# A radix-4 even half, a new front order and a table of vector shares in a kernel that mixes a spectral filter with a state-space recurrence

## The chip, the core and the metric

The kernel runs on one NeuronCore of one Trainium2 chip. Its engines work at the same time, each through a queue of its own in program order: TensorE (PE in the profile, its weight loads PEld), VectorE (DVE), ScalarE (ACT), GpSimd (POOL) and SyncE (SP), which here only issues DMAs. They meet through semaphores. The metric is device time of one execution in microseconds (us); lower is better. The time before is 340.28 us, the median of 3 runs (340.24 to 340.29).

## What is computed

One input x of 2048 tokens by 1024 channels goes two ways, and a gate per token mixes the results:

```python
g = sigmoid((x * gate_w).sum(-1, keepdims=True))
# way A: a filter in the two-dimensional spectrum
X = rfft2(x.astype(float32), axes=(-2, -1))
a = irfft2(X * (w_r + 1j * w_i), s=(S, D), axes=(-2, -1)).astype(bfloat16)
# way B: a diagonal complex recurrence over the tokens, P = 1024 states
Lam_bar = exp(dt * Lam);  B_bar = ((Lam_bar - 1.0) / Lam)[:, None] * Bmat
Bu = einsum("bld,pd->blp", x, B_bar)
h[t] = Lam_bar * h[t-1] + Bu[t]
b = 2.0 * einsum("blp,dp->bld", h, Cmat).real + x * Dskip
out = g * a + (1 - g) * b
```

Shapes: S = 2048, D = 1024; inputs and output are bfloat16.

## The kernel before, in words

**Way A** is done with matrix products. The *front* treats 16 row groups j = 0..15 of 128 tokens. For each, `turn_x(j)` (L663) transposes the group with 8 TensorE transposes into `pt`, and ScalarE copies it out into `xQ` (L667), from where way B reads x too. `fold(j)` (L670) makes on VectorE the sums and the differences of the lower and the upper 512 channels: two instructions of 512 elements (L674, L675) into `preT`. `fd(j)` (L342) is the transform along d: the sums go against a matrix for the even frequencies and the differences against one for the odd ones, 4 matmuls of 512 columns each (L346), and one copy of 1024 elements out of PSUM into `X1` (L349; on VectorE for j = 3, 5, 7, else on ScalarE). `s1(j)` (L352) is the first step of the transform along the tokens, 4 matmuls on half the rows (L358); its result `A1` is copied out by VectorE for j < 8 and by ScalarE from 8 on (L363) and goes to DRAM by a DMA of SP (L365, tile `turn_scratch`). From j = 8 on, `A1` lives in four rotating buffers, so A1 of j = 12 waits until the store of j = 8 has landed and until VectorE has kept a column of it (`keep_A1`, L371). `fd` and `s1` share two PSUM buffers (`psA`): each waits until what stood in its buffer two uses ago has been copied out.

**Way B** has 8 chunks c of 256 tokens. `unit(c, q)` (L301) yields two *halves*: 32 matmuls of 256 columns each (L308, tile `psu`), copied out by ScalarE (L310, tile `h`). A half needs its four transposed parts of B (`BT`, DMA transposes of SP, L207). After the second half, `recur` (L254) appends the chunk's recurrence as a list of pieces for VectorE: multiplications by tables of sines and cosines (L263, L266), additions, scans (L278). `vector(us)` (L321) takes pieces from this list, in order, until the sum of their listed costs reaches what is owed; `c_half(tb)` (L574), 16 matmuls against C and 4 for the skip term, first takes all pieces of its chunk that are left (`vector_until`, L330). So where `vector` is called and with how much sets where the recurrence stands in VectorE's queue. `early(tb)` makes output tiles 0..9 ahead, `own_tile` the last ones.

**The tables** come from `make_tab(jp)` for four groups jp (L210). Each is a chain that goes from VectorE (angles, L215; range reduction, L828, L830) to ScalarE (L832, L833, L835 and the scaled copies `t`, L226, L231) and back (tab, L232, L237). Its tiles have one buffer, so a table starts after the one before it has been read. It is cut by `yield`s into about four pieces, which the loop over the front hands out. Ahead of the tables, a small version of the same chain (`sincos` on `ang2`, L844) and some 24 tiny VectorE operations (L847 to L869) make the factors per state.

**The order around the change.** TensorE, VectorE and ScalarE run in the order in which the program is written; the DMAs of SP and POOL are ordered by the framework's scheduler. The front is a loop (L872) that calls `front()` for j = 0..15. `plan` gives for each j the order of F (`fd(j+1)`), S (`s1(j)`), T (the next `turn_x`) and f (the next `fold`), and `order` the loads that follow it: parts of B, later parts of C (L563, also DMA transposes of SP, which may only write where A1 of j < 8 was stored). A half of way B follows each j from 8 on, and `vector(4.2)` each from 9 on. `T2` (tile `raw`) is the matrix of `s1`, loaded in three parts. After the front come the middle part of way A (`step()`) with halves, `early` tiles and `vector` calls between its steps, and the closing loop. The first instruction after the front's last `s1` is the TensorE operation at L400.

Of the kernel before, what the change touches and what calls it, by code (L numbers as in the profile page):

```python
# [14 lines left out]
BF16 = mybir.dt.bfloat16  # L15
# [6 lines left out]
K = 512  # L22
H = K // 2
# [6 lines left out]
NSEP = 2  # L30

MAGIC = 12582912.0
INV2PI = float(1.0 / (2.0 * np.pi))
# [4 lines left out]
def _host_consts():  # L38
# [3 lines left out]
    for cls in range(2):  # L42
# [3 lines left out]
        G[cls, :, 1] = -np.sin(ang)  # L46
    G[0, :, 1, 0] = (-1.0) ** np.arange(K)

    n = np.arange(H)[None, :] + 0.5
# [40 lines left out]
    for h in range(2):  # L90
# [7 lines left out]
    return dict(  # L98
        G=b16(G.reshape(2, 4, P, K).transpose(2, 0, 1, 3)),
        Gi=b16(Gi.reshape(8, P, H).transpose(1, 0, 2)),  # L100
# [9 lines left out]
def kernel(  # L110
# [80 lines left out]
    fft = {}  # L191
    fft["G"] = pre.tile([P, 2, 4, K], BF16, name="G_sb")
    raw = t3p.tile([P, 6 * D], BF16, name="raw")
# [5 lines left out]
    def load_T2(a, b):  # L199
        nc.sync.dma_start(out=fft["T2"][:, a:b], in_=cT2[:, a:b])  # L200
# [117 lines left out]

    owed = [0.0]

    def vector(us):  # L321
# [15 lines left out]
    def gfnet():  # L337
# [4 lines left out]
        def fd(j):  # L342
            ps = psA.tile([P, 2, K], FP32, name="ps_fd", tag="ps")
            for cls in range(2):
                for d4 in range(4):
                    nc.tensor.matmul(ps[:, cls, :], lhsT=preTs[j][:, 4 * cls + d4, :], rhs=G_sb[:, cls, d4, :],  # L346
                                     start=(d4 == 0), stop=(d4 == 3))
            X1 = gta.tile([P, 2, K], BF16, name="X1")
            (nc.vector.tensor_copy if j in (3,5,7,) else nc.scalar.copy)(out=X1.rearrange("p r (i c) -> p r i c", c=2), in_=ps.rearrange("p c (r i) -> p r i c", r=2))  # L349
            X1s[j] = X1  # L350

        def s1(j):  # L352
            X1 = X1s.pop(j)
            psa = psA.tile([P, 2, K], FP32, name="ps_s1", tag="ps")
            for r in range(2):
                for g in range(2):
                    half = slice(64 * g, 64 * (g + 1))
                    nc.tensor.matmul(psa[:, g, :], lhsT=T2_sb[half, j, 64 - 64 * r:192 - 64 * r], rhs=X1[half, r, :],  # L358
                                     start=(r == 0), stop=(r == 1), tile_position=(64 * g, 0))
            A1 = CT[0][:, j, :].rearrange("p (g k) -> p g k", g=2) if j < 8 else A1_4[:, j % 4]  # L360
            if j in (8, 12):
                keep_A1(j - 4)
            (nc.vector.tensor_copy if j < 8 else nc.scalar.copy)(out=A1, in_=psa)  # L363
            A1s[j] = A1
            nc.sync.dma_start(out=t1_w[j], in_=A1)  # L365
# [294 lines left out]

    preTs = {}

# [7 lines left out]
    def fold(j):  # L670
        preTs[j] = gta.tile([P, 8, P], BF16, name="preT", bufs=3)
        lo, hi = (x_gjq[:, :, d:d + 4, :, j, :].rearrange("p c d g q -> p d g c q") for d in (0, 4))
        to = preTs[j].rearrange("p d (g c q) -> p d g c q", g=2, c=NCH)
        nc.vector.tensor_add(out=to[:, 0:4], in0=lo, in1=hi)  # L674
        nc.vector.tensor_sub(out=to[:, 4:8], in0=lo, in1=hi)  # L675

# [10 lines left out]
    load_x(0)  # L687
    for cls in range(2):
        nc.sync.dma_start(out=fft["G"][:, cls], in_=cG[:, cls])
    load_T2(0, 2)  # L690
# [3 lines left out]
    for i in range(3, 8):  # L694
        load_x(i)
    load_T2(8, 16)
    assert step() == "front"
# [68 lines left out]
    def halves(gen, n):  # L766
# [5 lines left out]
    order = {  # L772
        **{j: [(load_B, n)] for j, n in ((2, 1), (3, 1), (4, 1), (5, 2), (6, 2), (7, 2), (8, 2), (9, 2))},
        10: [(load_B, 3), (load_small,)],
        **{j: [(load_C, j - 11)] for j in range(11, 15)},
# [3 lines left out]

    plan = {0: "FSTfTf", 1: "TSFfT", 2: "TFfTS", 3: "TFfTS", 4: "TFfTS", 5: "TFfTS", 6: "TFfTS", 7: "TFfTS"}  # L780

    def front(pieces=0):
        j = at[0]
        at[0] += 1
        for what in plan.get(j, "fFS"):
            if what == "T":
                for r in rows:
                    turn_x(r)
                    break
            elif what == "f":  # L790
                for r in folds:
                    fold(r)
                    break
            elif what == "F":
                if j + 1 < 16:
                    fft["fd"](j + 1)
            else:
                fft["s1"](j)
        for load, *args in order.get(j, ()):
            load(*args)  # L800
        for _ in range(pieces):
            next(tables, None)
# [33 lines left out]

    front()

# [4 lines left out]
    c2c = sp.tile([P, 2, 8], FP32, name="c2c")  # L843
    for _ in sincos(sp, ang2, [P, 2, 8], s2c, c2c, "a2"):  # L844
        front()
    sth, cth = s2c[:, 0], c2c[:, 0]
# [25 lines left out]
    while at[0] < 16:  # L872
        j = at[0]
        front(0 if j < 4 else 1 if j < 6 else 2 if j < 10 else 3)
        if j >= 8:
            halves(ssm, 1)
        if j >= 9:
            vector(4.2)
        if j == 10:
            gate()  # L880
        if j == 15:
            for _ in tables:
                pass
            tctx.close()
        if j == 7:
            xctx.close()
            pools["u"] = ctx.enter_context(tc.tile_pool(name="psU", bufs=2, space=PSUM, reuse_waits="tile"))
        if j == 3:
            load_Wcols()
    for q in range(4, 8):  # L890
        load_C(q)
    for v, n in (("w", 4), ("a", 1), ("z", 2), ("q", 2), ("qn", 1), ("s2", 0), ("uv", 1)):
        assert step() == v
        for i in range(n):
            if v == "w" and i == 0:
                nc.vector.tensor_mul(out=fft["dgD"], in0=ident.unsqueeze(1).to_broadcast([P, 8, P]),
                                     in1=vecT[:, 3].unsqueeze(2).to_broadcast([P, 8, P]))
            if v == "w" and i == 3:
                gate_end()
            halves(ssm, 1)  # L900
            vector(3.0)
    for g in range(16):
        assert step() == "is1"
        assert step() == "uv"
        halves(ssm, 1)
        vector(3.3)
    halves(ssm, 1)
    vector(3.0)
    halves(ssm, 1)
    vector(3.0)  # L910
    for g in range(16):
        assert step() == "is2"
        if g == 12:
            after_ic()
        if g % 2:
            halves(ssm, 1)
        vector(2.0)
    for _ in ssm:
        vector(3.5)
    assert step() is None  # L920
# [17 lines left out]
    for _ in chain(unit(7, 0)):  # L938
        vector(4.0)
    for n in (1, 1):  # L940
        halves(last, 1)
        vector(4.0)
        close_early(n)
# [3 lines left out]
    for tb, counts in ((10, (1, 1)), (11, (1, 1)), (12, (1, 1)), (13, (1, 1)), (14, (0, 0)), (15, (0, 0))):  # L947
        for _, n in zip(own(tb), counts):
            vector(4.0)
            close_early(n)  # L950
            if not late:
                close(0)
# [31 lines left out]
```

## Time and profile before

| what | value |
|---|---|
| median of 3 runs | 340.28 us |
| the profiled execution, its own time | 340.26 us |
| its span, first to last instruction | 338.5 us |
| granted TensorE clock | 1.00 throughout |
| L346, the transform along d | 128 matmuls, 30.4 us busy |
| L674 and L675, the folds | 16 each, 460 and 416 ns on average |
| L349, X1 out of PSUM | 13 on ScalarE at 1013 ns, 3 on VectorE at 1217 ns |
| L363, A1 out of PSUM | 8 on VectorE at 1218 ns, 8 on ScalarE at 1020 ns |
| L667, a turned group out of PSUM | 16 on ScalarE at 1016 ns |
| L400, first after the front | starts at 86.86 us |

The profile is one execution. A row of a timeline gives the start and the length in us, the engine, the line of the program, the operation, what it writes and reads, the shape, and how many like it were merged; in square brackets stands how long the engine had been idle before it and what released it. Lengths of neighbours on one engine overlap a little, so what an instruction costs in a dense queue is the distance from its start to the next start. A matmul's listed length holds some 0.16 us of pipeline that the next one covers.

### The profile page before, as it was taken

Reading aid. Unit: us, or ns where it says so; the run is one execution under the profiler, and the core shown is the slowest. Engines: PE = TensorE matmul, PEld = TensorE weight load, DVE = VectorE, ACT = ScalarE, POOL = GpSimd, SP = SyncE. Lnnn points to the kernel's source line nnn. Section 1 sums busy time; section 2 is a strip of 40 time slices with the busy share of each in tenths; the row PEclk is TensorE's granted clock in tenths of the full one; section 3 lists DMA queues with packets and bytes.
Section 4 is the critical chain, followed back from the end, with each engine's and each line's share of the span. In section 5 each row is a group of like instructions: output and inputs, shape, how many; then the busy total and the mean of one; then the engine's idle time right before and its main releaser. Section 6 shows DMA issues by size and latency. Waiting matters only on the chain.

```text
span 338.5 us, 6167 instructions
## 1 busy us (share of the span) xinstructions
PE 327.9 (97%) x2446; PEld 212.0 (63%) x2446; DVE 283.5 (84%) x385; ACT 167.3 (49%) x211; POOL 32.7 (10%) x64
## 2 busy tenths in 40 slices
PE   8989899979999999999999999999999999999995
PEld 3445465656985574847566575869945876565552
DVE  2679948999999999999997999199699939999741
ACT  3697598836241245656557452546632243433510
POOL 1382011140000000000000000000000011121410
PEclk9999999999999999999999999999999999999999
DMA  7999999999890346899999955898114004556892
GB/s 268 404 200 144 244 220 213 129 202 263 261 230 11 95 123 145 254 243 282 259 270 242 218 174 151 225 188 217 62 33 122 35 4 71 102 86 124 131 194 102
DMA packets 83581, 58.71 MB, mean 173 GB/s; under 512 B 54328, under 2 KB 74304, under 8 KB 83424
## 3 DMA queue, kind: packets, MB, share of 16 engines
q1 hardware_dynamic: 80304, 55.64, 66.5%
q0 software_dynamic: 3168, 2.66, 8.3%
q8 instruction: 19, 0.31, 0.4%
q14 instruction: 10, 0.08, 0.1%
q10 hardware_dynamic: 80, 0.01, 0.0%
HBM read 30.49 MB, written 17.83 MB: 143 GB/s over the span
## 4 chain that ended last, share of the span: by engine, by line
PE 81%; DVE 13%; ACT 3%; issue 2%; ACTq 0%; DVEq 0%
PE ps_y L580 29%; PE psu L308 28%; PE ps_h L580 4%; PE ps_id L611 4%; PE ps_fd L346 3%; PE ps_is L519 2%; PE ps_is L494 2%; PE ps_s L470 2%; PE ps_is L495 2%; DVE CT L363 2%; PE ps_y L584 2%; DVE h L278 1%; DVE preT L674 1%; PE psw L684 1%; DVE preT L675 1%
## 5 line engine op out<-in xcount | busy, mean ns | idle before, releaser
L308 PE MATMUL psu<-xQ,BT 128*128 128x256 bf16 x1024 | 116.2, 273 | 0.8 <-ACT ye L598 0.5
L308 PEld LDWEIGHTS <-BT 128*128 128x128 bf16 x1024 | 99.0, 98 | 17.4 <-issue 4.5
L580 PE MATMUL ps_y<-CT,h 128*128 128x512 bf16 x448 | 101.3, 379 | 0.0
L580 PEld LDWEIGHTS <-h 128*128 128x128 bf16 x512 | 49.4, 98 | 55.3
L278 DVE TENSOR_TENSOR_SCAN h<-rz,h 128x1024 bf16<-128x1024 f32 x32 | 71.9, 2278 | 0.2
L310 ACT CAST h<-psu 128x1024 bf16<-128x1024 f32 x32 | 32.3, 1010 | 51.0 <-PE psu L308 51.0
L263 DVE TENSOR_TENSOR xQ<-h,tab 128x4096 bf16<-128x4096 bf16 x12 | 27.4, 2287 | 14.2 <-ACT h L310 14.2
L266 DVE TENSOR_TENSOR h<-h,tab 128x4096 bf16<-128x4096 bf16 (+1 forms) x20 | 37.3, 1864 | 0.8
L626 POOL DMA_DIRECT2D BT<-y_scratch x10 | 11.9, 1194 | 238.8 <-DVE BT L620 227.1
L598 ACT ACTIVATE ye<-ps_y,omg 128x512 f32<-128x512 f32 x20 | 12.7, 684 | 43.4 <-PE ps_y L584 35.7
L346 PE MATMUL ps_fd<-G_sb,preT 128*128 128x512 bf16 x128 | 30.4, 379 | 1.6 <-ACT X L349 1.0
L346 PEld LDWEIGHTS <-preT 128*128 128x128 bf16 x128 | 12.0, 97 | 15.5 <-issue 2.8
L472 ACT CAST X<-ps_s 128x1024 bf16<-128x1024 f32 x16 | 16.2, 1014 | 8.7 <-PE ps_s L470 8.7
L667 ACT COPY xQ<-pt 128x1024 bf16<-128x1024 bf16 x16 | 15.6, 1016 | 2.6 <-PE pt L666 2.5
L521 ACT CAST ZT<-ps_is 128x1024 bf16<-128x1024 f32 x16 | 15.5, 1024 | 2.2 <-PE ps_is L519 2.2
L497 ACT CAST C<-ps_is 128x1024 bf16<-128x1024 f32 x16 | 16.1, 1007 | 0.0
L611 PE MATMUL ps_id<-raw,ZT 128*128 128x256 bf16 x128 | 15.9, 273 | 0.0
L349 ACT CAST X<-ps_fd 128x1024 bf16<-128x1024 f32 x13 | 13.2, 1013 | 5.5 <-PE ps_fd L346 5.4
L580 PE MATMUL ps_h<-CT,h 128*128 128x512 bf16 x64 | 14.5, 379 | 0.0
L611 PEld LDWEIGHTS <-ZT 128*128 128x128 bf16 x128 | 12.4, 98 | 2.2
L674 DVE TENSOR_TENSOR preT<-xQ 128x512 bf16<-128x512 bf16 x16 | 7.4, 460 | 5.8 <-ACT xQ L667 5.8
L494 PE MATMUL ps_is<-X,raw 128*128 128x512 bf16 x32 | 12.1, 379 | 0.0
(189 smaller groups left out, 350.0 us busy)
## 6 DMA issues: line engine op xcount, KB each, us to landing
y_scratch<-ye SPq DMA_DIRECT2D x20, 256.0 KB, 2.7
CT<-in_A_x_dram SPq DMA_DIRECT2D x8, 512.0 KB, 5.6
Bb<-turn_scratch SPq DMA_DIRECT2D x16, 256.0 KB, 3.8
turn_scratch<-C SPq DMA_DIRECT2D x16, 256.0 KB, 4.5
raw<-turn_scratch SPq DMA_DIRECT2D x16, 256.0 KB, 4.7
Wb<-in_A_w_r_dram SPq DMA_DIRECT2D x32, 127.8 KB, 4.0
Wb<-in_A_w_i_dram SPq DMA_DIRECT2D x32, 127.8 KB, 3.8
out_dram<-BT SPq DMA_DIRECT2D x14, 256.0 KB, 2.6
```

What stands on the lines that cost most here:

```text
L263: nc.vector.tensor_mul(out=tmps["s"], in0=u[:, ::-1], in1=bc(i))
L266: nc.vector.tensor_mul(out=u, in0=u, in1=bc(i))
L278: nc.vector.tensor_tensor_scan(out=seg, data0=rz[:, js.start + j:js.start + j + 4].rearrange("p j t -> p (j t)"), data1=seg, initial=0.0, ...
L308: nc.tensor.matmul(psu[:, j, :], lhsT=BT[4 * q + j][:, ri, d8, :], rhs=xQ[:, c, d8, :], start=(d8 == 0), stop=(d8 == 7))
L310: nc.scalar.copy(out=hs[c][:, ri, 4 * q:4 * q + 4].rearrange("p b (q j) -> p b q j", j=32), in_=psu.rearrange("p b (j q) -> p b q j", j=32))
L346: nc.tensor.matmul(ps[:, cls, :], lhsT=preTs[j][:, 4 * cls + d4, :], rhs=G_sb[:, cls, d4, :], start=(d4 == 0), stop=(d4 == 3))
L472: nc.scalar.copy(out=X2, in_=ps2)
L494: nc.tensor.matmul(psc[:, h, :], lhsT=MT_sb[:, b, 64:192], rhs=UV[0][:, h, :], start=True, stop=False)
L497: nc.scalar.copy(out=C1.rearrange("p h (c i) -> p h c i", c=2), in_=psc.rearrange("p h (i c) -> p h c i", c=2))
L580: nc.tensor.matmul(psy, lhsT=hs[c][:, ri, jb, P * tq:P * (tq + 1)], rhs=CT[ri][:, jb, 512 * dh:512 * (dh + 1)], start=(i == 0), stop=False)
L611: nc.tensor.matmul(pse[:, slot, :], lhsT=ZT_t[:, i, tb, :], rhs=fft["Gi"][:, i, :], start=(kb == 0), stop=(kb == 1))
L667: nc.scalar.copy(out=x_gjq[:, :, :, :, j, :].rearrange("p c d g q -> p d c g q"), in_=pt.rearrange("p d (c q g) -> p d c g q", c=NCH, g=2))
```

## The change

The even half of the transform along d is split once more. The 512 sums are folded into 256 sums and 256 differences, and these go against two matrices of 256 columns: 4 matmuls of 512 columns (odd half, now first) and 4 of 256 columns. `fold` makes the differences first, then the sums into a tile of its own, then the second level; from j = 4 on, the second level is done for two groups at once, when the odd one of the pair is folded. The matrix `G` becomes smaller and is loaded odd part first.

The front is laid out anew: `plan` gives every j an order; all turns are done by j = 4 (before: j = 6); five `front()` calls stand ahead of the small `sincos` chain instead of one, and one stands within it; the PSUM of the turns is handed to way B after j = 5 instead of j = 7; halves of way B stand at j = 6..13 instead of 8..15; the tables are handed out four pieces per j from j = 6 on; the loads of B start at j = 1 and end at j = 7 (before: 2 to 10); the second half of `T2` is loaded after the B loads of j = 3 instead of in the beginning. A1 of j = 4 and X1 of j = 7 change from VectorE to ScalarE.

The amounts given to `vector` come one after another from a table `SHARE` of 71 numbers. Over the seven calls of the front they come to 23.5 (before 7 times 4.2), over the next eleven to 30.5 (before 33).

```diff
 
+SHARE = (
+    4, 5.2, 3.6, 5.9, 2.8, 1, 1, 2.2, 2.2, 3.7, 2.2, 3, 3, 3, 2.5, 3.5,
+    3, 2.2, 3.3, 3.3, 4.8, 3.3, 3.3, 3.3, 3.3, 3.3, 3, 2.6, 3, 3.3, 3.3, 3.3,
+    2.5, 3, 3.2, 3, 0, 2, 4, 2, 2, 2, 2.5, 2, 2, 1.5, 2, 2,
+    2, 2, 2, 2, 3.5, 3.5, 3.5, 4, 6, 4, 4, 2, 4, 4, 4.5, 4.5,
+    4.5, 4.5, 4.5, 4.8, 4.3, 4.3, 4.3,
+)
+
...
     G[0, :, 1, 0] = (-1.0) ** np.arange(K)
+    Ge = np.stack([G[0, :H, :, e::2] for e in range(2)])
+    Go = np.stack([G[1, :, :, e::2] for e in range(2)], axis=1)
...
     return dict(
-        G=b16(G.reshape(2, 4, P, K).transpose(2, 0, 1, 3)),
+        G=b16(np.concatenate([Go.reshape(4, P, 4 * K // 4).transpose(1, 0, 2).reshape(P, 4 * K),
+                              Ge.reshape(2, 2, P, H).transpose(2, 0, 1, 3).reshape(P, 4 * H)], axis=1)),
...
     fft = {}
-    fft["G"] = pre.tile([P, 2, 4, K], BF16, name="G_sb")
+    fft["G"] = pre.tile([P, 4 * K + 4 * H], BF16, name="G_sb")
...
     owed = [0.0]
+    share = iter(SHARE)
...
             ps = psA.tile([P, 2, K], FP32, name="ps_fd", tag="ps")
-            for cls in range(2):
-                for d4 in range(4):
-                    nc.tensor.matmul(ps[:, cls, :], lhsT=preTs[j][:, 4 * cls + d4, :], rhs=G_sb[:, cls, d4, :],
-                                     start=(d4 == 0), stop=(d4 == 3))
+            Go = G_sb[:, 0:4 * K].rearrange("p (d n) -> p d n", d=4)
+            Ge = G_sb[:, 4 * K:4 * K + 4 * H].rearrange("p (e d n) -> p e d n", e=2, d=2)
+            for d4 in range(4):
+                nc.tensor.matmul(ps[:, 1, :], lhsT=preTs[j][:, 4 + d4, :], rhs=Go[:, d4, :], start=(d4 == 0), stop=(d4 == 3))
+            for e in range(2):
+                for d2 in range(2):
+                    nc.tensor.matmul(ps[:, 0, H * e:H * (e + 1)], lhsT=preTs[j][:, 2 * e + d2, :], rhs=Ge[:, e, d2, :],
+                                     start=(d2 == 0), stop=(d2 == 1))
             X1 = gta.tile([P, 2, K], BF16, name="X1")
-            (nc.vector.tensor_copy if j in (3,5,7,) else nc.scalar.copy)(out=X1.rearrange("p r (i c) -> p r i c", c=2), in_=ps.rearrange("p c (r i) -> p r i c", r=2))
+            (nc.vector.tensor_copy if j in (3, 5) else nc.scalar.copy)(
+                out=X1.rearrange("p r (m e c) -> p r m e c", e=2, c=2),
+                in_=ps.rearrange("p c (e r m) -> p r m e c", e=2, r=2))
...
                 keep_A1(j - 4)
-            (nc.vector.tensor_copy if j < 8 else nc.scalar.copy)(out=A1, in_=psa)
+            (nc.vector.tensor_copy if j in (0, 1, 2, 3, 5, 6, 7) else nc.scalar.copy)(out=A1, in_=psa)
...
 
-    preTs = {}
+    preTs, pairs = {}, {}
...
     def fold(j):
-        preTs[j] = gta.tile([P, 8, P], BF16, name="preT", bufs=3)
+        if j % 2 == 0:
+            pairs["t"] = gta.tile([P, 2, 8, P], BF16, name="preT", bufs=2)
+            pairs["s"] = gta.tile([P, 2, 4, P], BF16, name="sums", bufs=1)
+        preTs[j] = pairs["t"][:, j % 2]
         lo, hi = (x_gjq[:, :, d:d + 4, :, j, :].rearrange("p c d g q -> p d g c q") for d in (0, 4))
-        to = preTs[j].rearrange("p d (g c q) -> p d g c q", g=2, c=NCH)
-        nc.vector.tensor_add(out=to[:, 0:4], in0=lo, in1=hi)
-        nc.vector.tensor_sub(out=to[:, 4:8], in0=lo, in1=hi)
+        apart = lambda t: t.rearrange("p d (g c q) -> p d g c q", g=2, c=NCH)
+        nc.vector.tensor_sub(out=apart(preTs[j])[:, 4:8], in0=lo, in1=hi)
+        nc.vector.tensor_add(out=apart(pairs["s"][:, j % 2]), in0=lo, in1=hi)
+        rs = slice(j % 2, j % 2 + 1) if j < 4 else slice(0, 2)
+        if j < 4 or j % 2:
+            s_lo, s_hi = pairs["s"][:, rs, 0:2], pairs["s"][:, rs, 2:4]
+            nc.vector.tensor_add(out=pairs["t"][:, rs, 0:2], in0=s_lo, in1=s_hi)
+            nc.vector.tensor_sub(out=pairs["t"][:, rs, 2:4], in0=s_lo, in1=s_hi)
...
     load_x(0)
-    for cls in range(2):
-        nc.sync.dma_start(out=fft["G"][:, cls], in_=cG[:, cls])
+    for part in (slice(0, 4 * K), slice(4 * K, 4 * K + 4 * H)):
+        nc.sync.dma_start(out=fft["G"][:, part], in_=cG[:, part])
...
         load_x(i)
-    load_T2(8, 16)
...
     order = {
-        **{j: [(load_B, n)] for j, n in ((2, 1), (3, 1), (4, 1), (5, 2), (6, 2), (7, 2), (8, 2), (9, 2))},
-        10: [(load_B, 3), (load_small,)],
+        1: [(load_B, 4)],
+        2: [(load_B, 2)],
+        3: [(load_B, 2), (load_T2, 8, 16), (load_Wcols,)],
+        **{j: [(load_B, 2)] for j in range(4, 8)},
+        10: [(load_small,)],
...
 
-    plan = {0: "FSTfTf", 1: "TSFfT", 2: "TFfTS", 3: "TFfTS", 4: "TFfTS", 5: "TFfTS", 6: "TFfTS", 7: "TFfTS"}
+    plan = {0: 'FTfSTf', 1: 'TFTfTS', 2: 'FTfTST', 3: 'TFTffST', 4: 'FTTfST', 5: 'fFS', 6: 'fFS', 7: 'ffFS', 8: 'FfS', 9: 'SfF', 10: 'SF', 11: 'fFS', 12: 'FS', 13: 'FS', 14: 'FS', 15: 'FS'}
...
 
-    front()
+    for _ in range(5):
+        front()
...
     c2c = sp.tile([P, 2, 8], FP32, name="c2c")
-    for _ in sincos(sp, ang2, [P, 2, 8], s2c, c2c, "a2"):
-        front()
+    turns = sincos(sp, ang2, [P, 2, 8], s2c, c2c, "a2")
+    next(turns)
+    front()
+    xctx.close()
+    pools["u"] = ctx.enter_context(tc.tile_pool(name="psU", bufs=2, space=PSUM, reuse_waits="tile"))
+    for _ in turns:
+        pass
...
         j = at[0]
-        front(0 if j < 4 else 1 if j < 6 else 2 if j < 10 else 3)
-        if j >= 8:
+        halves(tables, 1)
+        front(2)
+        if j in (6, 7, 8, 9, 10, 11, 12, 13):
             halves(ssm, 1)
+        halves(tables, 1)
         if j >= 9:
-            vector(4.2)
+            vector(next(share))
...
             gate()
-        if j == 15:
-            for _ in tables:
-                pass
-            tctx.close()
-        if j == 7:
-            xctx.close()
-            pools["u"] = ctx.enter_context(tc.tile_pool(name="psU", bufs=2, space=PSUM, reuse_waits="tile"))
-        if j == 3:
-            load_Wcols()
+    tctx.close()
...
             halves(ssm, 1)
-            vector(3.0)
+            vector(next(share))
...
         halves(ssm, 1)
-        vector(3.3)
+        vector(next(share))
     halves(ssm, 1)
-    vector(3.0)
+    vector(next(share))
     halves(ssm, 1)
-    vector(3.0)
+    vector(next(share))
...
             halves(ssm, 1)
-        vector(2.0)
+        vector(next(share))
     for _ in ssm:
-        vector(3.5)
+        vector(next(share))
...
     for _ in chain(unit(7, 0)):
-        vector(4.0)
+        vector(next(share))
...
         halves(last, 1)
-        vector(4.0)
+        vector(next(share))
...
         for _, n in zip(own(tb), counts):
-            vector(4.0)
+            vector(next(share))
...
```

## The prediction

> **What bounds the kernel now.** I read the busy times first, then the stretches of ten microseconds, then the chain of waits, then the timeline of the front.
>
> ```profile
> PE 327.9 (97%) x2446; PEld 212.0 (63%) x2446; DVE 283.5 (84%) x385; ACT 167.3 (49%) x211; POOL 32.7 (10%) x64
> 10.00:20.00 10.00, 9.14 (x81) 5.01 (x80) 6.86 (x17) 7.89 (x13) 5.00 (x20) 1.00 1.19 355
> 20.00:30.00 10.00, 9.13 (x77) 5.16 (x77) 9.75 (x35) 7.64 (x9) 5.70 (x10) 1.00 1.09 159
> 30.00:40.00 10.00, 8.64 (x61) 3.88 (x60) 9.93 (x20) 7.89 (x12) 1.94 (x4) 1.00 1.14 207
> 70.00:80.00 10.00, 8.30 (x62) 5.16 (x60) 9.86 (x12) 5.25 (x6) 1.37 (x7) 1.00 1.14 225
> 80.00:90.00 10.00, 10.00 (x105) 8.45 (x103) 9.55 (x20) 4.29 (x5) 0.00 (x0) 1.00 0.84 216
> ```
>
> The columns after the length are PE, PEld, DVE, ACT, POOL, the granted clock, the DMA share and GB/s. TensorE sets the time: 97%, and from 80 to 260 us each stretch of ten shows it 10.00 busy. Before 40 us it is not the bound: VectorE stands at 9.75 and 9.93 there, and the chain of waits goes through VectorE rows from 20 to 40 us. So whatever lets the front end earlier comes out whole at the end, as long as the later part keeps TensorE dense; and in the front both the TensorE work and the VectorE and ScalarE chain count.
>
> ```profile
> 35.04 1.22 DVE L363 CAST CT<-ps_s 128x1024 bf16<-128x1024 f32 x1
> 36.17 0.87 DVE L232 SCALAR_TENSOR_TENSOR tab<-cs_f,cr,t 128x256 bf16<-128x256 f32 x2
> 36.96 0.42 DVE L674 TENSOR_TENSOR preT<-xQ 128x512 bf16<-128x512 bf16 x1
> 37.30 0.41 DVE L675 TENSOR_TENSOR preT<-xQ 128x512 bf16<-128x512 bf16 x1
> 37.63 1.22 DVE L363 CAST CT<-ps_s 128x1024 bf16<-128x1024 f32 x1
> 39.78 0.61 PE L358 MATMUL ps_s<-X,raw 64*128 64x512 bf16 x4
> 40.32 3.67 PE L308 MATMUL psu<-xQ,BT 128*128 128x256 bf16 x32
> 43.82 1.89 PE L346 MATMUL ps_fd<-G_sb,preT 128*128 128x512 bf16 x8
> 60.33 0.61 DVE L215 TENSOR_SCALAR ang<-tau_f,thp 128x256 f32<-128x256 f32 x2
> 60.97 0.43 DVE L828 TENSOR_SCALAR rot_kk<-ang 128x512 f32<-128x512 f32 x1
> 61.44 0.69 DVE L830 TENSOR_TENSOR ang<-ang,rot_kk 128x512 f32<-128x512 f32 x1
> 62.16 0.63 ACT L832 ACTIVATE rot_kk<-ang 128x512 f32<-128x512 f32 x1 [0.82 <-DVE ang L830]
> 62.70 0.61 ACT L833 ACTIVATE sn_f<-ang 128x512 f32<-128x512 f32 x1
> 63.22 0.71 ACT L835 ACTIVATE cs_f<-rot_kk,chpi 128x512 f32<-128x512 f32 x1
> 63.83 0.89 ACT L226 ACTIVATE t<-sn_f,ci 128x256 f32<-128x256 f32 x2
> 64.63 0.89 ACT L231 ACTIVATE t<-cs_f,ci 128x256 f32<-128x256 f32 x2
> 72.81 0.61 PE L358 MATMUL ps_s<-X,raw 64*128 64x512 bf16 x4 [1.70 <-ACT A L363]
> ```
>
> From start to start: an A1 copy on VectorE 1.13 us, a fold 0.34 + 0.33, an s1 0.54, a half 3.50 (0.110 per 256 columns), and an fd (1.89 - 0.16)/8 = 0.216 per 512 columns. The table rows are one whole chain: 1.72 us of VectorE from the angles to the reduced range, 3.3 us of ScalarE after it. The last row is the one large stall of TensorE in the later front, 1.7 us.
>
> **TensorE work removed.** 4 of 8 matmuls per fd go from 512 to 256 columns: 4 x (0.216 - 0.110) = 0.43 us; an fd falls from 1.73 to 1.30, and 16 of them by 6.8 us. Up to the first operation behind the front (86.86 us) TensorE's work is 4.5 (warm-up) + 7.2 (turns) + 27.6 (fd) + 8.6 (s1) + 28.0 (8 halves) + 1.9 (gate, small ones) = 77.8 us, so 9.1 us idle. After the change the work is 71.0; the question is the idle time.
>
> [...]
>
> **VectorE work added.** Second level of the folds: 8 instructions of 256 elements (groups 0 to 3) and 12 of 512 (six pairs). No row has 256 elements in bfloat16; tiny operations take 0.17, the 512-element fold 0.34: I take 0.2, since most of a tiny one's time is not elements, and 0.34 for the pairs: 8 x 0.2 + 12 x 0.34 = 5.7 us. Ends: 5.4, or 11.0 with 0.34 and with 0.69 (float row L830 of 512 elements). VectorE gives up A1 of 4 and X1 of 7, 2.3 us, to ScalarE (0.95 each there). The new X1 copy reads four places of PSUM in turn instead of two; the nearest row is L349 itself, 1.01, taken; the far one is L714, 1.10 for half the elements, so 2.2 at worst, some 5 us on the ScalarE path below. A loss is more likely than a gain here, so the low end is 1.01.
>
> **The first part, j = 0 to 5.** Through ScalarE: fd(0) and fd(1) end 0.43 earlier each, so the copy of X1(1) starts at about 10.2 (11.06 before). Then stand 14 turns, X1 of 1, 2, 4 and A1 of 4: 18 x 0.955 = 17.2, to 27.4; 28 with small waits. X1 of 6, the table load (1.28) and the small sine and cosine (0.75) follow: 31. The tiny VectorE operations took 21.79 to 24.97, so 31 to 34.2, and the first table's range reduction is done at 36.0. VectorE's own sum to A1 of 5 (6 A1-sized copies, X1 of 3 and 5, ten folds at 1.05) ends near 29.7, so ScalarE is the later one. TensorE meanwhile does fd(7) at 29 (it needs X1 of 6 copied), s1(6), the first half from 30.9 to 34.4, fd(8) to 35.7. Then s1(7) needs A1 of 6, which VectorE reaches behind the tiny operations, the angles and fold(10): 36.0 + 0.75 + 1.15 = 37.9. **Stall 2.2.**
>
> **The tables, j = 6 to 9.** Four pieces per j make one table per j, a closed loop: range reduced, 3.3 of ScalarE with a half's copy inside (0.95), the last tab operation (0.45), next angles (1.72): 6.4 us. TensorE needs 1.30 + 0.54 + 3.50 = 5.34 per j. So the reductions end at 36.0, 42.4, 48.9, 55.3. A1 of 7 stands behind the second and two folds: 45.8, while TensorE is ready for s1(8) at 43.2. **Stall 2.6.** From j = 8 A1 is on ScalarE and TensorE finds what it needs: s1(9) at 49.9, s1(10) at 55.2.
>
> A wait is added: `preT` holds two pairs, so fold(12) waits for fd(9) (43.4, when VectorE is there at 43.9) and fold(14) for fd(11) (57.2, VectorE there at 55.3: 1.9 idle). Behind it stand the last tab, `vector(4)`, `vector(5.2)`, fold(15), `vector(3.6)`, then keep_A1 at 73.7 and so A1 of 12 at 74.7; s1(13) waits 0.4 for it. Also fd of an even group now waits for the odd group's fold; the last, fd(14) at 73, has fold(15) done at 70, cover 3 us; without it TensorE waits there. The gate adds 1.75, j = 11 to 13 go at 5.34 each, and j = 14 and 15 have no half to hide X1 of 15: 1.3 idle. The operation behind the front then starts at 82.5 instead of 86.86: **4.3 us earlier** (6.8 less work, 2.3 more idle).
>
> **What moves with it.** Each of the 14 early turns brings 8 transposes and one copy, counted above. On SP 16 B transposes move ahead: issued from 13.3 to 44.9 before, 2.0 us each, with some 5 to land. The halves now want 4 parts at 30.9, 8 at 38, 12 at 46, 16 at 52; the old pace gives 29, 37, 43, 50. It just holds. The A1 stores queue behind them as now; store 9 left at 74.0 and landed at 77.5, and A1 of 13 wants it at 76: hidden by the half that follows. T2's second part, behind eight transposes, is due at 45.8 and would be issued near 32. POOL's loads of two columns of W keep their j. C was issued by 73.9 and is first used at 101.5, then 97. All are costed at nothing; a microsecond late beyond that cover is a microsecond lost.
>
> **Behind the front.** The recurrence of chunks 0 and 1 has listed cost 50.8 and must be done before the third early tile; SHARE gives 51.8 by then, before it was 59.4. Between L400 and that tile VectorE has the 28.3 listed (27.2 by the rows, which run 4% under the list) and 9.1 of small work (dgD 1.2, the gate 0.9, the column's steps 5.6, the first products with W 1.4) against TensorE's 38 us (86.9 to 125.3 before), so it keeps up, with about 1.5 us to spare. In the filter steps a group costs VectorE 1.37 + 3.2 = 4.6, TensorE 4.8. No change at the end: the closing rows shift as they are.
>
> Sum, against the profiled execution's own 340.26 (span 338.5 and 1.8 around it; the median is 340.28, the same): 340.26 - 4.3 = **336.0**.
>
> **Rivals.** *A, the table loop does not hold TensorE* (VectorE reaches A1 of 6 and 7 in time): both stalls go, 336.0 - 4.8 = 331.2. For it: TensorE has work for 71 us only; against it: the order above puts the copies behind the angles. *B, the front gains little*: the dear ends of the folds or of X1 (+5), or tables that cost ScalarE more: 338 to 341. For it: VectorE is 98% busy from 20 to 40 us already. *C, slower: the B parts come late.* Place: the halves of j = 7 to 9. The first three transposes took 8.93 us, 3.0 each, beside the loads of x; at that pace the 16th is issued at 61 and lands at 66 instead of 52: 14 us of stall, 350. It decides where the 16th lands after 56.3 (52 + 4.3), 2.3 us per issue. Against it: the pace fell to 1.3 to 1.9 once x had landed. That the matmuls do not become shorter is excluded by the half's rows.
>
> **How the numbers follow.** Forecast (334 to 338) 0.51; A (330.5 to 334) 0.20; B (338 to 341) 0.15; C (over 341) 0.14. A measurement of this kernel tells 0.2%, 0.7 us, from no change. Faster takes the forecast, A and half of B: 0.79; same 0.05; slower C and the rest of B: 0.16. Leaving out the lower end of A (0.08) and the upper part of C (0.12) gives 332.4 to 341.4.
>
> **What would show it.** Right: L346 at some 64 x 0.216 + 64 x 0.110 = 20.9 us; TensorE idle ahead of s1 of 7 and 8, released by VectorE's A1; reductions 6.4 us apart; L400 at 82.5. Wrong: idle ahead of L308 released by BT (C), TensorE dense from 31 us on (A), or TensorE waiting for h at L580 (the late recurrence), which I gave no case of its own.

## The result and the profile after

The changed kernel takes 338.62 us (337.92 to 338.82, 4 runs) against 340.28 (340.24 to 340.39): ratio 0.9947, interval 0.993 to 0.9964. It is faster by 1.66 us, inside the range, where 4.3 was forecast; the time lies in the part that the prediction gave to rival B (338 to 341). Its profiled execution took 338.71 with a span of 336.9. The ratios here and below leave out executions over 1.5% above the fastest of their kernel (two of e9, one of e6).

The groups by line first: busy time, mean ns of one, then the idle time ahead of them and what ended it.

```profile
L359 PE MATMUL ps_fd<-G_sb,preT 128*128 128x512 bf16 x64 | 16.5, 380 | 1.2 <-ACT X L365 1.2
L376 PE MATMUL ps_s<-X,raw 64*128 64x512 bf16 x64 | 9.7, 380 | 5.1 <-DVE CT L381 4.5 <-ACT X L365 0.6
L362 PE MATMUL ps_fd<-G_sb,preT 128*128 128x256 bf16 x64 | 9.6, 273 | 0.0
```

L359 is the odd half of `fd`, L362 the even half, L376 `s1`. The work is as short as expected, but 4.5 us of idle time stand ahead of `s1`, released by VectorE's copies of A1 (L381). The stretches of ten microseconds (columns as in the prediction) show where:

```profile
30.00:40.00 10.00, 8.88 (x70) 6.12 (x70) 7.20 (x32) 6.48 (x12) 1.22 (x2) 1.00 1.00 225
40.00:50.00 10.00, 6.60 (x46) 4.55 (x44) 9.82 (x22) 7.34 (x12) 1.44 (x2) 0.88 1.18 217
50.00:60.00 10.00, 10.00 (x77) 6.87 (x76) 5.42 (x13) 9.36 (x16) 2.47 (x4) 0.94 1.02 211
80.00:90.00 10.00, 8.98 (x89) 6.79 (x88) 9.76 (x18) 4.47 (x6) 0.00 (x0) 1.00 0.93 236
```

From 40 to 50 us TensorE is 6.60 busy, and the granted clock, 1.00 everywhere in the profile of the kernel before, is 0.88 and then 0.94. A "10.00 busy" at a lower clock is not 10.00 of work (below, the same 32 matmuls take 5.33 us for 3.67): that is the trap of the third row. TensorE's timeline of this place:

```profile
37.93 0.61 PE L376 MATMUL ps_s<-X,raw 64*128 64x512 bf16 x4 [1.12 <-DVE CT L381]
38.47 3.67 PE L319 MATMUL psu<-xQ,BT 128*128 128x256 bf16 x32
41.97 1.03 PE L359 MATMUL ps_fd<-G_sb,preT 128*128 128x512 bf16 x4
42.84 0.60 PE L362 MATMUL ps_fd<-G_sb,preT 128*128 128x256 bf16 x4
46.84 0.61 PE L376 MATMUL ps_s<-X,raw 64*128 64x512 bf16 x4 [3.40 <-DVE CT L381]
47.38 5.33 PE L319 MATMUL psu<-xQ,BT 128*128 128x256 bf16 x32
52.65 0.60 PE L376 MATMUL ps_s<-X,raw 64*128 64x512 bf16 x4
85.31 0.16 PE L418 MATMUL Wrev_ps<-Wc,JP_sb 128*128 128x4 bf16 x1 [0.40 <-ACT A L381]
```

s1(8) waits 3.40 us for A1 of 7, and the same 32 matmuls that took 3.67 us at 38.47 take 5.33 at 47.38: the record of the granted clock has 0.5 from 47.70 for 3.413 us. What VectorE did meanwhile, and GpSimd's two rows of that time below it:

```profile
43.65 0.42 DVE L701 TENSOR_TENSOR preT<-sums 128x512 bf16<-128x512 bf16 x1
43.98 0.83 DVE L695 TENSOR_TENSOR preT<-xQ 128x512 bf16<-128x512 bf16 x1
44.74 0.82 DVE L696 TENSOR_TENSOR sums<-xQ 128x512 bf16<-128x512 bf16 x1
45.48 1.21 DVE L381 CAST CT<-ps_s 128x1024 bf16<-128x1024 f32 x1
```

```profile
43.85 0.69 POOL L233 CAST tab<-sn_f 128x512 bf16<-128x512 f32 x1 [5.31 <-ACT sn_f L861]
44.49 0.80 POOL L239 CAST tab<-cs_f 128x512 bf16<-128x512 f32 x1
```

fold(12), two instructions that last 0.42 each in the fold before it (42.52, 42.85), lasts twice as long beside the two table casts (1.50 us from its start to the start of the copy behind it, where 0.67 was said), and A1 of 7 stands behind it. The first operation behind the front (now L418) starts at 85.31, against 86.86 before and 82.5 forecast: 1.55 us earlier, nearly the whole 1.66 of the median. Nothing is lost or won behind the front. Of the 2.8 us against the forecast, 2.75 are there at s1(9) already (52.65 for 49.9).

One part of this has nothing to do with the change: the first `fd` of this execution starts at 7.40, that of the kernel before at 6.96, and in the profiles of the variants below it starts anywhere from 6.53 to 7.58. The whole early front moves with it (e8 below: first `fd` 0.87 earlier, s1(8) 0.87 earlier). Counted from the first `fd`, the front is 2.0 us shorter than before (77.91 to L418, for 79.90).

### The profile page after: what moved, and what is told of

Read it like the earlier page. It is cut to its first block, busy times and chain, and to the rows that moved or that the text cites. A ratio compares the mean times of both kernels' runs of the same rounds, so it can differ in the third digit from the quotient of the medians.

```text
span 336.9 us, 6192 instructions
## 1 busy us (share of the span) xinstructions
PE 323.7 (96%) x2446; PEld 213.7 (63%) x2446; DVE 286.7 (85%) x403; ACT 169.3 (50%) x213; POOL 32.4 (10%) x64
## 4 chain that ended last, share of the span: by engine, by line
PE 83%; ACT 5%; DVE 5%; SPq 4%; issue 1%; DMA 1%; ACTq 0%; DVEq 0%
PE ps_y L598 29%; PE psu L319 28%; PE ps_h L598 4%; PE ps_id L629 4%; SPq L583 3%; PE ps_fd L359 2%; PE ps_is L537 2%; PE ps_is L513 2%; PE ps_is L512 2%; PE ps_s L488 2%; PE ps_y L602 2%; PE pt L684 2%; PE psw L710 1%; ACT xQ L685 1%; SPq L411 1%
## 5 line engine op out<-in xcount | busy, mean ns | idle before, releaser
L319 PE MATMUL psu<-xQ,BT 128*128 128x256 bf16 x1024 | 117.9, 275 | 0.8 <-ACT ye L616 0.5
L319 PEld LDWEIGHTS <-BT 128*128 128x128 bf16 x1024 | 100.1, 99 | 17.4 <-issue 3.2
L359 PE MATMUL ps_fd<-G_sb,preT 128*128 128x512 bf16 x64 | 16.5, 380 | 1.2 <-ACT X L365 1.2
L365 ACT CAST X<-ps_fd 128x1024 bf16<-128x1024 f32 x14 | 14.2, 1013 | 3.0 <-PE ps_fd L362 2.9
L376 PE MATMUL ps_s<-X,raw 64*128 64x512 bf16 x64 | 9.7, 380 | 5.1 <-DVE CT L381 4.5
L496 DVE TENSOR_TENSOR V<-X,Wb 128x1024 bf16<-128x1024 bf16 x16 | 10.9, 680 | 1.6 <-issue 1.5
```

Of the source, the lines that this page charges most:

```text
L319: nc.tensor.matmul(psu[:, j, :], lhsT=BT[4 * q + j][:, ri, d8, :], rhs=xQ[:, c, d8, :], start=(d8 == 0), stop=(d8 == 7))
L359: nc.tensor.matmul(ps[:, 1, :], lhsT=preTs[j][:, 4 + d4, :], rhs=Go[:, d4, :], start=(d4 == 0), stop=(d4 == 3))
```

## The experiments

The theory: the front lost 2.8 us against the forecast, about 1.0 by a later s1(8) and 1.7 by the half clock that followed it. The rivals: the new order or the amounts carry the gain and radix-4 none; the pause alone is the cost; something behind the front gives the time back. Twelve kernels ran; all medians in us, ratios against the kernel before as it ran beside them.

| run | median (range) | ratio, interval |
|---|---|---|
| e1_warm | 337.25 (336.99 to 340.61) | 0.991, 0.9888 to 0.9933 |
| e2_copies_first | 337.6 (336.94 to 337.82) | 0.991, 0.9891 to 0.993 |
| e3_radix4_alone | 346.42 (345.97 to 347.13) | 1.0174, 1.0153 to 1.0196 |
| e4_order_alone | 340.43 (340.27 to 340.92) | 0.9985, 0.9964 to 1.0006 |
| e5_old_amounts | 344.54 (343.88 to 345.73) | 1.011, 1.0083 to 1.0137 |
| e6_loop | 338.44 (335.75 to 341.14) | 0.9919, 0.9889 to 0.9949 |
| e7_pool_stores | 337.55 (336.54 to 338.08) | 0.9893, 0.9868 to 0.9919 |
| e8_warm6 | 338.51 (336.89 to 338.57) | 0.9922, 0.9896 to 0.9948 |
| e9_first_warm | 339.52 (336.66 to 343.19) | 0.9941, 0.9906 to 0.9976 |
| e10_x_first | 337.08 (336.83 to 341.39) | 0.9896, 0.9845 to 0.9948 |
| e11_act_casts | 337.22 (336.68 to 337.7) | 0.988, 0.9842 to 0.9919 |
| e12_a9_scalar | 335.73 (335.25 to 336.09) | 0.9837, 0.9796 to 0.9879 |

**Filling the pause.** e1_warm is the changed kernel with fourteen matmuls ahead of s1(8):

```diff
+    def warm(n):
+        psw = pools["u"].tile([P, 2, K], FP32, name="psw_u", tag="psu")
+        for i in range(n):
+            nc.tensor.matmul(psw[:, i % 2, :], lhsT=ident, rhs=fft["G"][:, 0:K], start=True, stop=True)
...
+                if j == 8:
+                    warm(14)
                 fft["s1"](j)
```

> The changed kernel with 14 matmuls of 512 columns more on TensorE (3.0 us, their result is used by nothing), put in the pause of 3.6 us ahead of s1 of j = 8; everything else stays, VectorE's copy of A1 of 7 included. Theory 'clock' (the pause of TensorE made the granted clock fall to 0.5 for 3.4 us, and the half behind it took 5.33 us for that reason): the half takes 3.5 to 3.7 us, the granted clock is 1.00 throughout, the first operation behind the front starts at 83.6 instead of 85.3 and the time is 336.9, 1.7 below the changed kernel's 338.6. Rival 'data' (the half was slow because parts of B or PSUM came late, or because of memory traffic beside it): the half stays at 5.3 us and the time at 338.6.

```profile
42.77 3.19 PE L813 MATMUL psw_u<-G_sb,ident 128*128 128x512 bf16 x14
46.34 0.61 PE L376 MATMUL ps_s<-X,raw 64*128 64x512 bf16 x4 [0.39 <-DMA BT<-in_B_B_im_dram]
46.88 3.67 PE L319 MATMUL psu<-xQ,BT 128*128 128x256 bf16 x32
```

With matmuls that nobody reads in the pause, the half behind it takes 3.67 us again, and four of the six runs lie at 336.99 to 337.45, some 1.5 under the changed kernel. A fifth, 338.96, has a mean clock of 1.000 and was not profiled. The profiled execution is the slowest, 340.61; it has a half clock at 86.68 behind two pauses (1.61 and 1.22 us), of which the changed kernel has none of the first and 0.62 of the second. e9 below shows their cause.

e8_warm6 has `warm(6)` right behind fd(9), so that some 2.1 us of the pause stay open.

> As e1_warm, but with 6 added matmuls (1.3 us) instead of 14, right behind the transform of 9: 2.2 us of the pause stay. [...] Rival 'data': 338.6 in all.

```profile
42.40 1.46 PE L813 MATMUL psw_u<-G_sb,ident 128*128 128x512 bf16 x6
45.97 0.61 PE L376 MATMUL ps_s<-X,raw 64*128 64x512 bf16 x4 [2.11 <-DVE CT L381]
46.51 3.67 PE L319 MATMUL psu<-xQ,BT 128*128 128x256 bf16 x32
```

The result is two-valued: 336.89 and 337.52 with a mean granted clock of 1.000, and four runs at 338.5 to 338.57 with 0.995. In the profiled execution, one of the first kind, L418 starts at 82.88, 0.4 from the forecast, with the long folds (0.83 and 0.82) still there; its early start gives 0.87 of this. From the first `fd` to L418 it takes 76.35 us, the changed kernel 77.91: the clock is worth 1.56 here, about half of 3.413. The two kinds of time are 1.0 to 1.7 apart, so with some 2.1 us left open the clock falls in four executions and holds in two; what decides between them was not settled.

**The long folds.** e11_act_casts:

```diff
-        nc.gpsimd.tensor_copy(out=tab[:, 1, js, :], in_=sn_f)
+        (nc.scalar.copy if jp == 1 else nc.gpsimd.tensor_copy)(out=tab[:, 1, js, :], in_=sn_f)
```

> The changed kernel with the two casts of the second table (43.85 to 45.3 us on GpSimd) on ScalarE; nothing else is changed. Theory (the folds beside those casts take 0.8 instead of 0.42 us because of them): fold(12) 0.42 + 0.42 us, A1 of 7 some 0.8 earlier, the pause ahead of s1(8) 2.6 as predicted, and the time 0.8 less, 337.8; if the clock does not fall at 2.6 us, 336.2. Rival (the folds are slow for another reason, as the loads in flight): rows of 0.8 stay, pause 3.4, 338.6.

The edit as it ran moves only the first of the two casts; the second stays on GpSimd. VectorE, GpSimd and TensorE in its timelines:

```profile
44.16 0.42 DVE L695 TENSOR_TENSOR preT<-xQ 128x512 bf16<-128x512 bf16 x1
44.49 0.42 DVE L696 TENSOR_TENSOR sums<-xQ 128x512 bf16<-128x512 bf16 x1
44.82 1.22 DVE L381 CAST CT<-ps_s 128x1024 bf16<-128x1024 f32 x1
```

```profile
44.63 0.75 POOL L239 CAST tab<-cs_f 128x512 bf16<-128x512 f32 x1 [5.93 <-ACT cs_f L863]
```

```profile
46.19 0.61 PE L376 MATMUL ps_s<-X,raw 64*128 64x512 bf16 x4 [2.59 <-DVE CT L381]
46.73 3.67 PE L319 MATMUL psu<-xQ,BT 128*128 128x256 bf16 x32
```

Both folds are back at 0.42, and the pause is 2.59 us: the "Stall 2.6" of the prediction. Counted from the first `fd`, s1(8) comes 0.83 earlier than in the changed kernel (38.61 for 39.44). The second cast starts while a fold runs, and this time the cast is the longer one (0.75, alone 0.61). The clock held in this execution; in three of the six runs its mean is 0.995, and these are the slower ones (337.35 to 337.70 against 336.68 to 337.10). The median, 337.22, lies between the two that were expected.

**The copies ahead of the turns.** e2_copies_first changes the plan of two j, so that A1 comes ahead of the second fold:

```diff
-    plan = {0: 'FTfSTf', 1: 'TFTfTS', 2: 'FTfTST', 3: 'TFTffST', 4: 'FTTfST', 5: 'fFS', 6: 'fFS', 7: 'ffFS', 8: 'FfS', 9: 'SfF', 10: 'SF', 11: 'fFS', 12: 'FS', 13: 'FS', 14: 'FS', 15: 'FS'}
+    plan = {0: 'FTfSTf', 1: 'TFTfTS', 2: 'FTfTST', 3: 'TFTffST', 4: 'FTTfST', 5: 'fFS', 6: 'FSf', 7: 'FSff', 8: 'FfS', 9: 'SfF', 10: 'SF', 11: 'fFS', 12: 'FS', 13: 'FS', 14: 'FS', 15: 'FS'}
```

> The changed kernel with s1 (and so VectorE's copy of A1) ahead of the folds in the plan of j = 6 and 7. Theory 'order of VectorE' (A1 of 6 and 7 stand behind folds that nobody needs yet): s1 of 8 starts near 43.7 instead of 46.8, its pause is 1.1 us, the clock does not fall, and then the table loop (6.4 to 7 us a round) holds TensorE at s1 of 10, which waits for X1 of 10 near 56.4 instead of 58.1: time 336.9. Rival 'all of it' (nothing else holds TensorE): 334.7. Rival 'no matter' (A1 waits for the angles and the small operations, not for the folds): 338.6.

```profile
55.17 1.03 PE L376 MATMUL ps_s<-X,raw 64*128 64x512 bf16 x4 [2.31 <-ACT X L365]
56.14 1.89 PE L359 MATMUL ps_fd<-G_sb,preT 128*128 128x512 bf16 x4
57.82 0.97 PE L362 MATMUL ps_fd<-G_sb,preT 128*128 128x256 bf16 x4
```

s1(8) moves up to 42.94 with a pause of 1.01. What the tables lack comes out two j later: s1(10) waits 2.31 us for X1 of 10, and the rows behind it last twice as long (1.89 for 1.03), half clock again. 1.0 us won, of 2.8 lost; 0.7 less than expected.

Two edits of e2 tried to win the rest. e9_first_warm adds `warm(9)` ahead of s1(10); e10_x_first turns the plan of j = 9 from 'SfF' to 'FSf', so that X1 of 10 is copied ahead of A1 of 9.

> The order of e2_copies_first with nine matmuls of 512 columns, whose result nobody reads, ahead of s1(10), where that kernel's TensorE paused 2.31 us and its clock then fell to 0.5 for 3.4 us. Clock theory: no half clock at 55 us, 1.65 us less than the 337.6 of e2_copies_first: 335.9. Rival (the pause itself is the cost, the clock comes after it for another reason): 337.6, or more if the nine matmuls hold up s1(10).

> e2_copies_first with fd(10) and its copy X1(10) issued ahead of s1(9) and its copy A1(9). On ScalarE X1(10) then ends at 54.1 instead of 55.0, so the pause ahead of s1(10) is 1.4 instead of 2.3 us. Theory (pauses up to 1.7 leave the clock alone): no half clock, 337.6 - 0.9 - 1.65 = 335.1. Rival (ScalarE's order does not set s1(10), or the clock falls at 1.4 too): 336.7 to 337.6.

In e9 the clock holds at 55 us and the pause there is 0.37, yet its median is 339.52 where 335.9 was expected, and its executions lie up to 6.5 us apart. Its profiled execution (340.01) shows why, first SP's queue, then ScalarE, then TensorE:

```profile
65.95 0.66 SPq L383 DMA_DIRECT2D turn_scratch<-A  x1
66.65 9.23 SPq L583 DMA_TRANSPOSE CT<-in_B_C_re_dram  x5
75.99 1.94 SPq L383 DMA_DIRECT2D turn_scratch<-A  x3
```

```profile
81.38 1.01 ACT L381 CAST A<-ps_s 128x1024 bf16<-128x1024 f32 x1 [3.96 <-DMA turn_scratch<-A]
```

```profile
82.44 0.61 PE L376 MATMUL ps_s<-X,raw 64*128 64x512 bf16 x4 [1.29 <-ACT A L381]
84.27 0.61 PE L376 MATMUL ps_s<-X,raw 64*128 64x512 bf16 x4 [1.23 <-ACT X L365]
```

The A1 stores stand in SP's queue between the transposes of C, five of which take 9.23 us. Three stores leave only at 76; A1 of 13 waits 3.96 us for its buffer, two pauses follow within 3 us, and a half clock from 85.03. The changed kernel's first A store left at 58.5 us; here it left at 65.95, as the scheduler had set it behind three transposes of C that follow it there. e1's slow execution is the same case (first store at 66.2, A1 of 13 waiting 4.27).

e10's median is 337.08, 0.5 under e2 where 2.5 was expected. In its profiled execution, 341.39, the pause at s1(10) is 1.67 and the clock falls all the same (0.5 from 55.71), and the late stores come on top, with a second half clock from 86.43. The expectation that a pause up to 1.7 leaves the clock alone is wrong. Two of its runs, at 337.0 and 337.1, have a mean clock of 0.999, three at 336.83 to 337.14 one of 0.995: in these the half clock costs nothing that shows, and where the time went was not profiled and stays open.

**Parts alone.** e3_radix4_alone is the kernel before with the smaller matrix, `fd` and the X1 copy of the change, the second level of the folds made for each group at once. e4_order_alone is the changed kernel with the old `fold`, `G` and `fd`, and five `preT` buffers. e5_old_amounts is the changed kernel with `SHARE` set to what was there before:

```diff
-SHARE = (
-    4, 5.2, 3.6, 5.9, 2.8, 1, 1, 2.2, 2.2, 3.7, 2.2, 3, 3, 3, 2.5, 3.5,
...
+SHARE = (4.2,) * 7 + (3.0,) * 11 + (3.3,) * 16 + (3.0,) * 2 + (2.0,) * 16 + (3.5,) * 3 + (4.0,) * 16
```

> The kernel before with the radix-4 even half alone (second level of the fold for each group by itself, old order, old amounts). Theory 'VectorE holds the early front': L346's work falls by 6.8 us, but VectorE, 98% busy from 20 to 40 us, gets 6.4 us more, 4 of them before 40 us, and the first half starts later than 40.3: time 339.5 to 341. Rival 'TensorE's work counts whole': 333.5.

> The changed kernel with the old radix-2 transform and fold (order, loads and amounts as changed; five buffers of preT, so that no fold waits for a transform). Theory 'same stalls': the copies of A1 of 6 and 7 still hold TensorE at j = 7 and 8, pauses shorter by what fd is longer (0.43 each) and by the missing second level, so the clock may hold; TensorE has 6.8 us more work: 338.5 to 339.5. Rival 'the order serves the short transform only': 341 or more.

> The changed kernel with the old amounts in the table (4.2, 3.0, 3.3, 2.0, 3.5, 4.0 as before). Theory 'amounts are second order': up to j = 11 they come to nearly the same (12.6 for 12.8), so the pause at s1 of 8 and the clock stay as they are; over j = 12 to 15 VectorE gets 6 us more recurrence, so the small steps behind the front stand later: 338.6 to 340. Rival 'the amounts carry the gain': 340.3 or more. Rival 'they do nothing': 338.6 within 0.3.

Radix-4 in the old order is slower by 6 us, with all of its TensorE saving; neither expectation had that. VectorE and TensorE at the worst place (here L380 is `keep_A1`, L367 `s1`):

```profile
73.66 0.68 DVE L294 TENSOR_TENSOR h<-h,su 128x1024 bf16<-128x1024 bf16 x1
74.26 0.42 DVE L684 TENSOR_TENSOR preT<-xQ 128x512 bf16<-128x512 bf16 x1
75.46 0.18 DVE L380 COPY Acol<-A 128x8 bf16<-128x8 bf16 x1
```

```profile
76.78 1.04 PE L367 MATMUL ps_s<-X,raw 64*128 64x512 bf16 x4 [4.70 <-ACT A L372]
77.75 5.52 PE L311 MATMUL psu<-xQ,BT 128*128 128x256 bf16 x32
```

The column of A1 is kept behind the recurrence and the fold in VectorE's queue; A1 of 12 waits for it, TensorE stands still for 4.70 us, and the clock is 0.5 for 6.83 us from 74.75 on, as it was earlier in this kernel for 3.41 us from 26.96, at a pause of 2.23. The pauses, not the clock, are most of it: another execution with a mean clock of 0.994 takes 345.97, this one with 0.985 takes 346.08. The order alone neither gains nor loses (its longest pause near the tables is 1.27, the clock stays at 1.0), where 338.5 to 339.5 was expected. So the parts do not add up: +6.0 and 0.0 alone, -1.66 together.

With the old amounts the front ends almost as in the changed kernel (the operation of L418 at 85.69), and the time goes behind it:

```profile
108.34 0.57 PE L442 MATMUL zps<-Bcol,K_sb 32*128 32x16 bf16 x16 [4.16 <-DVE Bcol L435]
108.84 5.89 PE L592 MATMUL ps_y<-CT,h 128*128 128x512 bf16 x16
```

VectorE reaches the small copy `Bcol`, which the change had at 102.03, only at 108.08, behind recurrence pieces; the clock is 0.5 for 6.83 us from 106.62 on. The amounts are not of second order: without them the change would be slower than the kernel before by 1.1%.

**Towards a better version.** e6_loop puts the first table's angles ahead of the tiny VectorE operations, copies A1 of 8 and 9 on VectorE and takes A1 ahead of the folds; e7_pool_stores is e6 with the A1 stores of j = 8 to 11 on GpSimd's queue; e12_a9_scalar is e7 with A1 of 9 back on ScalarE. The edit of e12, against the changed kernel:

```diff
-            (nc.vector.tensor_copy if j in (0, 1, 2, 3, 5, 6, 7) else nc.scalar.copy)(out=A1, in_=psa)
+            (nc.vector.tensor_copy if j in (0, 1, 2, 3, 5, 6, 7, 8) else nc.scalar.copy)(out=A1, in_=psa)
-            nc.sync.dma_start(out=t1_w[j], in_=A1)
+            (nc.gpsimd if 8 <= j < 12 else nc.sync).dma_start(out=t1_w[j], in_=A1)
...
-    plan = {0: 'FTfSTf', 1: 'TFTfTS', 2: 'FTfTST', 3: 'TFTffST', 4: 'FTTfST', 5: 'fFS', 6: 'fFS', 7: 'ffFS', 8: 'FfS', 9: 'SfF', 10: 'SF', 11: 'fFS', 12: 'FS', 13: 'FS', 14: 'FS', 15: 'FS'}
+    plan = {0: 'FTfSTf', 1: 'TFTfTS', 2: 'FTfTST', 3: 'TFTffST', 4: 'FTTfST', 5: 'fFS', 6: 'FSf', 7: 'FSf', 8: 'FSff', 9: 'SF', 10: 'SFf', 11: 'fFS', 12: 'FS', 13: 'FS', 14: 'FS', 15: 'FS'}
...
+    tables = chain(*(make_tab(jp) for jp in range(4)))
+    halves(tables, 1)
...
-        halves(tables, 1)
-        front(2)
+        front(3)
```

> The changed kernel with the first table's angles ahead of the small operations, each table's last copies ahead of the copy of the half, s1 ahead of the folds at j = 6 to 10, and A1 of 8 and 9 copied by VectorE. Theory 'VectorE's order makes the pauses': pauses of TensorE at s1 of 7 and 8 under 1 us, no fall of the clock, the operation behind the front at 80.7 and the time 334.0 to 335.0. Rival 'SP takes over' (A1 of 12 to 14 wait for the stores of 8 to 10, which leave SP behind the C transposes at 69 to 75): 336 to 337, with pauses at s1 of 13 to 15. Rival 'the B parts are late': idle ahead of the halves of j = 7 to 9.

> The kernel of e6_loop with the stores of A1 of 8 to 11 on GpSimd's DMA queue instead of SP's. If SP holds the end of the front in e6_loop: the pauses at s1 of 13 to 15 go and the time is 1 to 2 us below e6_loop's. [...]

> e7_pool_stores with A1 of 9 on ScalarE. Its two pauses were 1.54 (ahead of fd(10)) and 2.31 us (ahead of fd(11)), both on VectorE's A1. Theory: the second goes, as VectorE no longer holds A1 of 9 behind the angles, no half clock: 335.0 to 336.0. Rival (A1 of 9 waits as long on ScalarE, behind the sine, the cosine and the half's copy): 337.5 as e7_pool_stores.

In e6 the pauses at s1(7) and s1(8) are gone, two new ones of 1.55 and 1.91 us stand ahead of fd(10) and fd(11), behind A1 of 8 and 9 on VectorE, and its runs range over 5 us, with a median 3.4 above the forecast of 335 at most; in its profiled execution three stores leave together at 75.63, A1 of 13 waits 4.87 us for one of them, and a second half clock follows from 86.04. The stores on GpSimd's queue take this wait and the spread away (1.5 us in e7, its median 0.9 below e6's). e12 loses the second pause too; its timeline and stretches:

```profile
46.14 0.60 PE L376 MATMUL ps_s<-X,raw 64*128 64x512 bf16 x4
48.29 1.02 PE L359 MATMUL ps_fd<-G_sb,preT 128*128 128x512 bf16 x4 [1.55 <-DVE A L381]
```

```profile
40.00:50.00 10.00, 8.45 (x68) 5.74 (x66) 9.90 (x20) 8.11 (x16) 3.17 (x5) 1.00 1.16 201
50.00:60.00 10.00, 8.68 (x74) 6.67 (x73) 7.65 (x17) 8.18 (x14) 2.49 (x4) 1.00 1.13 242
```

The clock is 1.00, L418 starts at 82.08, and the time is 335.73 in a range of 0.84 us: 1.6% under the kernel before, and faster than the change.

## Why the prediction had the place right and the size wrong

- **TensorE work removed: right.** An `fd` is 0.87 us of L359 and 0.44 of L362, 1.31 against 1.30 said. The listed busy time, 16.5 + 9.6 = 26.1 against 30.4, shows 4.3 less; the other 2.5 of the 6.8 is the 0.16 us by which a matmul's listed length (380 and 273 ns) is longer than the spacing from start to start (0.218 and 0.110 us); this overlap, at the end of a stretch, now stands twice in each of 16 `fd`. The 20.9 us given as a sign was a sum from start to start and could not be read in that column.
- **VectorE work added: right.** Second-level folds of 512 elements follow each other by 0.34, of 256 by 0.21 (in e3); the X1 copy is 1013 ns.
- **The first part: right.** First half at 31.85 (30.9 said), first reduction done at 36.1 (36.0), s1(7) at 37.93 (37.9). That it fits to 0.1 is in part luck: this execution started 0.44 later than the kernel before, which the walk could not know. The pause came as 1.22 ahead of fd(7) and 1.12 ahead of s1(7), where 2.2 ahead of s1(7) was said.
- **The tables, "Stall 2.6" at s1(8): the step that failed.** The walk had the place, the releaser and the order. Two of its terms were wrong. It gave fold(12) 0.34 + 0.33, and beside GpSimd's casts it took 1.50. And it counted the pause as lost time only, the clock at nothing: the half behind it, said to take 3.50, took 5.33 at a clock of 0.5. Of the 2.8 us by which L418 was later than said (85.31 for 82.5), 1.0 stands at s1(8) (46.84 for 45.8) and 1.7 behind it, the clock's. The 1.0 is 0.8 from the folds and 0.4 from the late start, less 0.2 by which the rest of the walk was too long. e11 takes the folds' part away and finds a pause of 2.59; e1 and e8 take the clock's part away. The reductions came 6.5, 7.4 and 6.8 apart (6.4 said). That it was visible beforehand is half true: L674 had a row of 0.83 us at 70.42 in the kernel before, beside a GpSimd cast. The clock was not to be seen in that profile: the longest late pause there, 1.70, had left it at 1.00. Later executions of the same kernel show it: three that ran beside e8 took 342.05 to 342.33 at a mean clock of 0.994.
- **preT, keep_A1: right in kind.** fold(14) waited 3.3 for `fd` (1.9 said), `keep_A1` came at 76.0 (73.7 said), late with the whole front; s1(13), said to wait 0.4 for it, follows its `fd` at 77.64 without a pause.
- **The moved DMAs at nothing: right for this kernel, with little cover.** B came in time (the only wait on it is 0.4). The A1 stores were hidden: store 9 left at 69.44, and in e8's profile, whose front ends 2.4 earlier, at 71.98. In e1 and e9 the scheduler's order on SP's queue is another, store 9 leaves at 76.34 and 75.99, and A1 of 13 waits for it. So the cover hangs on an order that a small edit moves.
- **Behind the front: right, and by the amounts.** Gain at L418 1.55, in all 1.66; with the old amounts 5.9 us more.
- **The rivals.** B (338 to 341) named the figure but not the cause: X1 and the folds, but for fold(12), were as cheap as taken. C did not occur; A's condition did not either.

## What to carry to other kernels

Where TensorE is the bound and another engine makes it pause for some 2 us, price the clock as well as the pause: here a half-clock stretch cost up to 1.7 us more, less or nothing where another engine held TensorE anyway (e3, perhaps e10), and in e8, with 2.1 us of pause, and in e11, with 2.6, the mean clock is 0.995 in some executions and 0.999 or 1.000 in others. Walk the copy that frees a PSUM buffer through the queue of the engine that makes it, and let it stand ahead of work with slack; each wait removed shows the next, so follow the chain (VectorE's copy, ScalarE's copy, then SP's stores) to its end. Two parts of a change that use each other's slack have no price of their own: radix-4 alone was 1.7% slower, the order alone nothing.

## What the runs showed of the hardware

- **The clock.** In the changed kernel the half clock lasted 3.413 us (from 47.70); in the other traces it came in one such stretch or, in e3 and e5, in two, 6.83. It came in or behind pauses of TensorE of 3.40 (the changed kernel), 4.70 and 2.23 (e3), 4.16 (e5), 2.31 (e2, e7), 1.91 (e6) and 1.67 (e10, with another 0.30 behind it), and behind two pauses close together, 1.29 and 1.23 within 3 us (e9), 1.61 and 1.22 (e1). With 1.55 (e12), 1.70 (the kernel before), 2.11 (the profiled execution of e8) and 2.59 (that of e11) the rows around the pause show 1.00. So the length of the pause alone does not tell: 1.67 brought the half clock and 2.59 did not, and of the six executions of e8 two have a mean clock of 1.000 and four one of 0.995. What decides was not settled.
- **What a half-clock stretch costs.** In the rows behind s1(8) 1.7 us (5.33 for 3.67). Between executions of one kernel with and without it: 1.0 to 1.7 in e8, 1.0 to 1.5 in e7, 0.25 to 1.0 in e11, nothing that shows in e10 and e3. These times also hold the differing start of up to 1 us.
- **Folds beside GpSimd casts** last 0.83 instead of 0.42 us (some 0.75 instead of 0.34 from start to start) in the rows where the cast had started first: at 43.98 and 44.74 in the changed kernel, at 70.42 in the kernel before. In e11 the fold at 44.49 started ahead of the cast at 44.63; it took 0.42, and the cast 0.75 instead of 0.61.
